# A decode kernel's second-layer queries spread between score groups, and one V half kept in the buffer

## The chip, the cores and the metric

The kernel runs on one core of a Trainium2 chip. The metric is device time in microseconds (us); lower is better. Kernels are compared only within the same rounds. A ratio is the mean time of one kernel's fast runs over that of the other's in the same rounds, so it is not quite the ratio of the medians that are quoted beside it.

## The reference, cut to what matters

Four blocks in a chain over eight batch rows, one token each: attention with a KV cache, an MLP block, and the same two again with the same weights and the same cache.

```python
def _A_ref(x, k_cache, v_cache, wq, wo):      # 8 rows, 16 query heads, 8 KV heads, 4096 keys, 256 wide
    q = (x @ wq) ...
    scores = einsum(q, k) * 256 ** -0.5
    o = einsum(softmax(scores), v)
    return o @ wo
x = x + A(layernorm(x));  x = x + B(layernorm(x))     # B: layernorm, two small MLPs
x = x + A(layernorm(x));  x = x + B(layernorm(x))     # the same K and V once more
```

One row's K for one head is 2 MiB, and so is its V. They are far too large to hold, and both layers need them, so loading them is the work.

## The kernel before

The cache goes through a buffer of 15 slots of 1 MiB; one load is "half" of a head's K or V. K of five heads per row (ten slots) is kept from the first layer to the second, so it is loaded and transposed once. V is loaded twice.

```python
KEEP_K = 5
KEEP_V = 0
NFILL = 2
...
def load_half(cache, b, h, half):
    i = free_slots.pop(0)
    ...  # one DMA of 1 MiB, waits for the last readers of slot i
...
def mid(b, first_head, heads):        # between the layers of one row
    mlp(x1T[:, :, b:b + 1], ...)      # x1T: the row after the first attention
    norm(x2T[:, :, b:b + 1], ...)
    groups = [[heads[0]], heads[1:]]  # query matmuls of head 1, then of the other seven
    for gr in groups:
        for h in gr: pe(lambda t, h=h: q_mms(t, range(4 * h, 4 * h + 4), 1, False), 16, ...)
        for h in gr: dv(...)          # copy the queries out of the bank psC
...
for b in range(B):
    mid(b, l2_heads[0], l2_heads + free_heads)
    if b + 1 < B: layer1(b + 1, free_heads[:NFILL])   # next row's heads 0, 1 fill the serial stretch
    layer2(b, l2_heads[:2])                           # kept heads 7, 6
    if b + 1 < B: layer1(b + 1, free_heads[NFILL:])   # next row's head 2
    layer2(b, l2_heads[2:])                           # kept heads 5, 4, 3
    layer2(b, free_heads)                             # cut: the last two rows order this differently
    if b + 1 < B: layer1(b + 1, kept_heads)           # next row's heads 3 to 7
```

A scheduler inside the kernel orders each engine's work once, at build time. The matmuls of `mid` have the highest priority, so PE does all of them before it turns to the first second-layer scores.

Of the kernel before, what the change touches and what calls it, by code (L numbers as in the profile page):

```python
# [18 lines left out]
RSQRT_MAGIC = 0x5F1FFFF9  # L19
RSQRT_STEPS = ((0.703952253, 1.681914091), (0.5, 1.5000003))  # L20
KEEP_K = 5
KEEP_V = 0
REP = 24
LAG = 1
NFILL = 2
FILL_EV = "ev"
PV0 = 128
PV1 = PV0 + DH
QW, HW, YW = 16, 24, 24
# [295 lines left out]
def bass_interleave_layers__gqa_block_cached__mixer_s_mlp__decode_kernel(  # L325
# [20 lines left out]
    plan = Plan()  # L346
# [72 lines left out]
    psC = nc.alloc_psum_tensor("psC", [P, 512], f32)  # L419
# [11 lines left out]
    def bcast(ap, shape, axis):  # L431

        dims = [list(x) for x in ap.ap]
        dims.insert(axis, [0, shape])
        return bass.AP(tensor=ap.tensor, offset=ap.offset, ap=dims)
# [8 lines left out]
    def dma_once(name, parts, keys, at):  # L444

        for i, (dst, src, nbytes) in enumerate(parts):
            dma(name, dst, src, nbytes, nc.alloc_semaphore(f"s_{name}{i}"), 16, [keys[i]],
                at - 0.5)
# [16 lines left out]
    YB = ["yb"]  # L465
# [12 lines left out]
    def const_b(gp):  # L478
# [5 lines left out]
            rd=["ident_f"], wr=["ident_b"])  # L484

    def const_c(v):
# [7 lines left out]
            wr=["sel"])  # L494

    for i in range(2):
        plan.op("dve", lambda v, i=i: v.memset(psS[i][:, PV0:PV0 + DH], 0.0), 0.3, "const",
                wr=[("pz", i)], banks=[("S", i)])
# [4 lines left out]
    def dv(fn, dur=0.13, rd=(), wr=(), banks=(), name="chain", prio=None):  # L503
        if prio is None:
            prio = CH + len(plan.ops)
        return plan.op("dve", fn, dur, name, rd=rd, wr=wr, banks=banks, prio=prio)

    def pe(fn, n, rd=(), wr=(), banks=(), name="chain", prio=None):
        if prio is None:
            prio = CH + len(plan.ops)  # L510
        d = 0.06 + 0.026 * n
        return plan.op("pe", fn, (d, d, 20 * n), name, rd=rd, wr=wr, banks=banks, prio=prio)
# [65 lines left out]
    def q_mms(t, mts, n, first):  # L578

        last = None  # L580
        w_ = QW if n == 1 else n
        for mt in mts:
            hq, c = mt // 2, mt % 2
            for kc in range(4):
                if kc < 3:
                    w = wq_sb[:, kc, hq * 256 + c:hq * 256 + 256:2]
                    r = yb[:, kc, 0:n]
                else:
                    o = (hq % 8) * 256
                    w = wqx_sb[:, o + c:o + 256:2]  # L590
                    r = yb[:, 3 if hq < 8 else 4, 0:n]
                if n == 1:
                    r = bcast(r, w_, 1)
                last = t.matmul(psC[:, mt * w_:(mt + 1) * w_], w, r, start=(kc == 0), stop=(kc == 3))  # L594
        return last

    WQ = ["wq0", "wq1", "wq2", "wqx0", "wqx1"]
# [62 lines left out]
    def flush(n):  # L660
        while len(pend) > n:
            pend.pop(0)()

    def pair(layer, b, h, kept_k, kept_v, keep_k, keep_v, lag=None):
# [126 lines left out]
        pend.append(back)  # L791
        flush(LAG if lag is None else lag)

# [22 lines left out]
                    wr=[("s", i, pc)], banks=[("T", bank)])  # L816
        a.tbank = v.tbank = bank

    def mid(b, first_head, heads):

        mlp(x1T[:, :, b:b + 1], ("x1", b), 1, x2T[:, :, b:b + 1], [("x2", b)])
        norm(x2T[:, :, b:b + 1], ("x2", b), 1, False)
        q = q2T[b % 2]
        groups = [[heads[0]], heads[1:]]
        for gr in groups:
            for h in gr:
                pe(lambda t, h=h: q_mms(t, range(4 * h, 4 * h + 4), 1, False), 16, rd=YB + WQ,
                   wr=["psC"], banks=["C"])
            lo, hi = min(gr), max(gr)
            for h in gr:  # L830
                dv(lambda v, h=h: v.tensor_copy(
                    q[:, 4 * h:4 * h + 4].rearrange("p (c j) -> p c j", c=2),
                    psC[:, 4 * h * QW:(4 * h + 4) * QW:QW].rearrange("p (j c) -> p c j", c=2)),
                   rd=["psC"], wr=[("q2", b, h)], banks=["C"])


    dma_once("x", [(x_row[:, 0:D], A_x[:, 0, :], 7168)], ["xr0"], 0)
# [1 line left out]
    def load_wq():  # L839
        dma_once("wq", [(wq_sb[:, kc, :], A_wq[kc * P:(kc + 1) * P, :], 1 << 20)  # L840
                        for kc in range(3)], ["wq0", "wq1", "wq2"], 2)
        dma_once("wqx", [(wqx_sb[0:64, :], A_wq[384:D, 0:2048], 1 << 19),
                         (wqx_sb[64:P, :], A_wq[384:D, 2048:4096], 1 << 19)], ["wqx0", "wqx1"], 2)

    def load_rest():
        dma_once("wo", [(wo_sb[:, 0:32 * D].rearrange("p (t n) -> p t n", n=D),
                         A_wo.rearrange("(t m) n -> m t n", m=P), 3670016)], ["wo0"], 6)
        dma_once("w3", [(w3_sb[:, kc, :], B_w3[kc * P:(kc + 1) * P, :], 458752)
                        for kc in range(3)], ["w30", "w31", "w32"], 18)
        dma_once("w3x", [(w3x_sb[0:64, :], B_w3[384:D, 0:896], 114688 * 2),  # L850
                         (w3x_sb[64:P, :], B_w3[384:D, 896:1792], 114688 * 2)], ["w3x0", "w3x1"], 18)
        dma_once("w4", [(w4_sb[:, 0:14 * D].rearrange("p (t n) -> p t n", n=D),
                         B_w4.rearrange("(t m) n -> m t n", m=P), 1605632)],
                 ["w40"], 20)
# [25 lines left out]
    free_heads = list(range(HKV - KEEP_K))  # L880
    kept_heads = list(range(HKV - KEEP_K, HKV))
    l2_heads = kept_heads[::-1]

    def layer1(b, heads):
        for h in heads:
            kk = h in kept_heads
            nv = KEEP_V if h == HKV - 1 else 0
            keep_v = [nv > 1, nv > 0]
            pair(0, b, h, None, None, yes if kk else no, keep_v)

    def layer2(b, heads):
        for h in heads:
            kk, kv = store.pop((0, b, h))
            pair(1, b, h, kk, kv, no, no)

    load_wq()
    load_rest()
    first_queries()
    layer1(0, free_heads + kept_heads)
    flush(0)  # L900
    for b in range(B):
        mid(b, l2_heads[0], l2_heads + free_heads)
        ev_eng[0] = FILL_EV
        if b + 1 < B:
            layer1(b + 1, free_heads[:NFILL])
        else:
            layer2(b - 1, free_heads)
        ev_eng[0] = "ev"
        layer2(b, l2_heads[:2])
        if b + 1 < B:  # L910
            layer1(b + 1, free_heads[NFILL:])
        layer2(b, l2_heads[2:])
        if b != B - 2:
            layer2(b, free_heads)
        if b + 1 < B:
            layer1(b + 1, kept_heads)
        flush(0)
# [4 lines left out]
    def ot(t):  # L922
        last = None
        for kc in range(4):
# [6 lines left out]
       rd=["psC"], wr=["o_row"], banks=["C"])  # L931
# [3 lines left out]
            wr=["done"], dma=(s_out, 16), prio=10 ** 6)  # L935
# [65 lines left out]
```

## Time and profile before

| | before |
|---|---|
| time, median of the first three runs | 1197.31 us |
| profiled span | 1196.5 us |
| HBM read | 463.54 MB, 432 loads of K and V |
| row period, from x1T to the next x1T, first six | 142.6 us |
| x1T to first second-layer scores | 22.4 to 25.3 us |

In the lines of the profile, PE is the matmul engine and PEld its loading of weights; DVE, ACT and POOL are the vector, scalar and GpSimd engines; SP issues the loads. L441 is line 441 of the kernel.

From the page of the kernel before: rate in 40 slices, bytes per queue, and what was read.

```profile
GB/s 348 409 398 418 320 413 416 417 414 348 417 416 418 385 372 417 418 416 359 390 416 417 418 325 401 417 415 418 346 417 417 417 399 350 417 417 366 345 415 155
q1 hardware_dynamic: 69344, 463.58, 96.1%
q8 instruction: 167, 2.74, 0.9%
HBM read 463.54 MB, written 0.01 MB: 387 GB/s over the span
```

The rate stands at 415 to 418 GB/s and falls once per row. That is a memory-bound kernel with eight dips. From the waits of the DMA queue (what the next load waited for; us in total, times, longest):

```profile
SPq L441 <- PE psS L697: 359.2, 117, 8.6
SPq L441 <- PE psS L737: 354.8, 141, 9.2
SPq L441 <- PE psT L805: 103.5, 50, 4.3
```

The loads wait for scores (L697) and value products (L737), which give slots back. Between the dips that costs nothing, since other loads are still in flight. In the dips it does. Here are ten-us windows of the second row, counted from x1T at 262.7 us; the columns are the length, the busy time of PE, PEld, DVE, ACT and POOL (with instructions), the granted clock, the DMA share (a packet counts whole where it starts, so 1.01 is possible) and GB/s.

```profile
252.70:262.70 10.00, 8.22 (x188) 6.03 (x186) 3.94 (x12) 1.23 (x5) 0.75 (x2) 1.00 1.01 415
262.70:272.70 10.00, 10.00 (x199) 9.89 (x198) 7.04 (x27) 3.50 (x7) 0.35 (x1) 1.00 0.96 377
272.70:282.70 10.00, 8.68 (x223) 7.81 (x222) 5.53 (x24) 2.02 (x10) 1.15 (x3) 1.00 0.85 287
282.70:292.70 10.00, 8.81 (x225) 7.33 (x221) 2.12 (x14) 0.76 (x5) 0.75 (x2) 0.53 0.99 373
292.70:302.70 10.00, 10.00 (x260) 8.73 (x256) 4.37 (x14) 2.79 (x8) 0.75 (x2) 0.96 1.00 415
```

In the dip PE is busy for 10.00 and then 8.68 of ten us: it transposes and scores the next row's first K halves and does the serial chain of norm, MLP, norm and queries. Slots come back when PE is done with their last readers. The timeline of the kernel before gives the two ends of the chain (start, length, engine, line, operation):

```profile
262.75 0.18 DVE L787 TENSOR_TENSOR x1T<-acc,psW 128x5 bf16<-128x5 f32 x1 [0.82 <-PE psW L775]
...
285.63 0.56 PE L697 MATMUL psS<-q2T,kv 128*128 128x48 bf16 x10
```

### The profile page before, as it was taken

Reading aid. Unit: us, or ns where it says so; the run is one execution under the profiler, and the core shown is the slowest. Engines: PE = TensorE matmul, PEld = TensorE weight load, DVE = VectorE, ACT = ScalarE, POOL = GpSimd, SP = SyncE. Lnnn points to the kernel's source line nnn. Section 1 sums busy time; section 2 is a strip of 40 time slices with the busy share of each in tenths; the row PEclk is TensorE's granted clock in tenths of the full one; section 3 lists DMA queues with packets and bytes.
Section 4 is the critical chain, followed back from the end, with each engine's and each line's share of the span. In section 5 each row is a group of like instructions: output and inputs, shape, how many; then the busy total and the mean of one; then the engine's idle time right before and its main releaser. Section 6 shows DMA issues by size and latency. Waiting matters only on the chain.

```text
span 1196.5 us, 46172 instructions
## 1 busy us (share of the span) xinstructions
PE 1005.6 (84%) x21301; PEld 861.9 (72%) x21301; DVE 509.1 (43%) x1632; ACT 274.3 (23%) x847; POOL 97.9 (8%) x270
## 2 busy tenths in 40 slices
PE   4878889889898887999789797888888888789787
PEld 4766877778677776777677686776877677678665
DVE  3433435444344443445344343444434453345333
ACT  0222213221132211332123211232223221132121
POOL 0000010000110011000110001000010000100110
PEclk9998889998899988999899988999889997899888
DMA  9999899999999999999999989999999999999893
GB/s 348 409 398 418 320 413 416 417 414 348 417 416 418 385 372 417 418 416 359 390 416 417 418 325 401 417 415 418 346 417 417 417 399 350 417 417 366 345 415 155
DMA packets 69536, 466.52 MB, mean 390 GB/s; under 512 B 7120, under 2 KB 13152, under 8 KB 13664
## 3 DMA queue, kind: packets, MB, share of 16 engines
q1 hardware_dynamic: 69344, 463.58, 96.1%
q8 instruction: 167, 2.74, 0.9%
q14 instruction: 25, 0.20, 0.0%
HBM read 463.54 MB, written 0.01 MB: 387 GB/s over the span
## 4 chain that ended last, share of the span: by engine, by line
PE 53%; DMA 34%; DVE 5%; issue 4%; SPq 3%; POOL 1%; ACT 0%
DMA kv<-in_A_v_cache_dram 20%; PE psT L805 18%; PE psS L697 14%; DMA kv<-in_A_k_cache_dram 14%; PE psS L737 8%; PE psW L775 4%; SPq L441 3%; PE psT L941 2%; DVE oS L751 2%; DVE oS L749 2%; PE psC L640 1%; PE psS L759 1%; PE psC L594 1%; PE psC L534 1%; PE psC L616 1%
## 5 line engine op out<-in xcount | busy, mean ns | idle before, releaser
L805 PE MATMUL psT<-ident_f,kv 128*128 128x128 f32 x2816 | 383.4, 284 | 11.4 <-DMA kv<-in_A_k_cache_dram 8.3
L805 PEld LDWEIGHTS psT<-ident_f,kv 128*128 128x128 f32 x2816 | 315.3, 145 | 25.6 <-DMA kv<-in_A_k_cache_dram 13.7
L813 DVE COPY kv<-psT 128x512 f32<-128x512 f32 x379 | 260.4, 691 | 171.2 <-PE psT L805 168.4
L814 ACT COPY kv<-psT 128x512 f32<-128x512 f32 x325 | 190.3, 586 | 517.9 <-PE psT L805 517.6
L737 PE MATMUL psS<-kv,pT 128*2 128x256 bf16 x4096 | 167.4, 289 | 45.2 <-DMA kv<-in_A_v_cache_dram 38.5
L697 PE MATMUL psS<-q2T,kv 128*128 128x48 bf16 x4096 | 145.6, 192 | 23.0 <-issue 22.8
L717 ACT ACTIVATE pT<-psS,nb 128x32 bf16<-128x32 f32 x256 | 73.2, 296 | 365.0 <-DVE nb L711 365.0
L697 PEld LDWEIGHTS psS<-q2T,kv 128*128 128x128 bf16 x4096 | 133.7, 103 | 31.7 <-issue 29.4
L697 PE MATMUL psS<-q1T,kv 128*128 128x48 bf16 x4096 | 143.2, 183 | 5.4 <-issue 4.9
L697 PEld LDWEIGHTS psS<-q1T,kv 128*128 128x128 bf16 x4096 | 130.1, 97 | 22.8 <-issue 17.6
L737 PEld LDWEIGHTS psS<-kv,pT 128*2 128x2 bf16 x4096 | 78.9, 85 | 75.5 <-DMA kv<-in_A_v_cache_dram 45.0
L709 POOL PARTITION_ALL_REDUCE gm<-pm x128 | 45.4, 354 | 893.5 <-DVE pm L707 845.6
L707 DVE TENSOR_REDUCE pm<-psS 128x2 f32<-128x64 f32 x128 | 28.7, 224 | 182.9 <-PE psS L697 182.2
L941 PE MATMUL psT<-ident_b 128*128 128x256 bf16 x614 | 100.3, 288 | 1.9 <-issue 1.9
L759 PEld LDWEIGHTS psS<-sel,oS 128*128 128x128 bf16 x512 | 23.9, 98 | 105.6 <-DVE oS L751 103.8
L775 PEld LDWEIGHTS psW<-oT,wo_sb 128*128 128x128 bf16 x2560 | 79.9, 97 | 23.2 <-DVE oT L765 11.9
L759 PE MATMUL psS<-sel,oS 128*128 128x2 bf16 x512 | 32.4, 167 | 74.7 <-DVE oS L751 67.7
L775 PE MATMUL psW<-oT,wo_sb 128*128 128x24 bf16 x2560 | 90.0, 183 | 6.0 <-issue 5.0
L749 DVE CAST oS<-psS 128x256 bf16<-128x256 f32 x128 | 54.1, 423 | 74.7 <-PE psS L737 72.3
L941 PEld LDWEIGHTS psT<-ident_b 128*128 128x128 bf16 x614 | 49.6, 100 | 22.9 <-issue 17.6
L722 POOL PARTITION_ALL_REDUCE Db<-rs x128 | 51.1, 399 | 173.4 <-ACT pT L717 173.4
L751 DVE TENSOR_TENSOR oS<-psS,oS 128x256 bf16<-128x256 f32 x128 | 54.3, 424 | 3.3
(83 smaller groups left out, 461.2 us busy)
## 6 DMA issues: line engine op xcount, KB each, us to landing
kv<-in_A_v_cache_dram SPq DMA_DIRECT2D x256, 1024.0 KB, 17.9
kv<-in_A_k_cache_dram SPq DMA_DIRECT2D x176, 1024.0 KB, 20.9
wo_sb<-in_A_wo_dram SPq DMA_DIRECT2D x1, 3584.0 KB, 32.9
wq_sb<-in_A_wq_dram SPq DMA_DIRECT2D x3, 1024.0 KB, 11.3
w_sb<-in_B_w_dram SPq DMA_DIRECT2D x1, 1568.0 KB, 23.8
w_sb<-in_B_w_dram SPq DMA_DIRECT2D x3, 448.0 KB, 24.4
wqx_sb<-in_A_wq_dram SPq DMA_DIRECT2D x2, 256.0 KB, 14.9
w3x_sb<-in_B_w_dram SPq DMA_DIRECT2D x2, 112.0 KB, 20.1
```

The source lines that it names most:

```text
L697: last = t.matmul(ps[:, 2 * i:2 * i + 2 * REP], a[:, c:256:2], bcast(rhs(c), REP, 1), start=(c == 0), stop=(c == 1))
L717: return a.activation(pT[nr][:, :, :].rearrange("p i j -> p j i")[:, jj, :], sview[:, jj, :], ACT.Exp, bias=nb[nr][:, jj:jj + 1], scale=IN ...
L722: plan.op("pool", lambda gp: gp.partition_all_reduce(Db[nr][:, :], rs[nr][:, :], P, RO.add), 0.5, "sum", rd=[("rs", nr, 0), ("rs", nr, 1)] ...
L737: last = t.matmul(ps[g4:g4 + 2, PV0:PV0 + DH], pT[nr][:, i, :], slot_ap(s_, s * 256, 256), start=(i < 4), stop=(i >= 28), skip_group_check ...
L749: plan.op("dve", lambda v: v.tensor_copy(oS[:, 0, :], po), 0.36, "o", rd=[("pv", par, x) for x in range(4)], wr=["oS0"], banks=[bk], prio=hi)
L751: plan.op("dve", lambda v: v.tensor_tensor(oS[:, 1, :], po, oS[:, 0, :], ALU.subtract), 0.36, "o", rd=["oS0"] + [("pv", par, x) for x in r ...
L759: last = t.matmul(ps[:, PV1 + 2 * c:PV1 + 2 * c + 2], oS[:, w, c * P:(c + 1) * P], sel[:, :], start=(w == 0), stop=(w == 1))
L775: last = t.matmul(psW[:, mt * YW:(mt + 1) * YW], dup(wo_sb, 2 * (2 * h + j) + c, mt), bcast(oT[nr][:, c, j:j + 1], YW, 1), start=(k == 0), ...
L805: last = t.transpose(psT[bank][:, s * P:(s + 1) * P], src, ident_f[:, :])
L813: return e.tensor_copy(dst, psT[bank][:, :])
L814: return e.copy(dst, psT[bank][:, :])
L941: last = t.matmul(psT[bank][:, 256 * i:256 * i + 256], ident_b[:, :], bcast(ident_b[:, :], 2, 1), start=True, stop=True)
```

## The change

The intent by its title is to shorten the chain: only two heads' queries (32 matmuls) are computed ahead of the first scores, and the other six heads' follow one by one between the score groups. The diff also sets `KEEP_V` to 1. The second V half of the last kept head (head 7) then stays in its slot until the second layer, which saves one load per row (424 loads instead of 432) and leaves four slots to rotate in the serial stretch instead of five.

```diff
-KEEP_V = 0
+KEEP_V = 1
+QFIRST = 2
...
-    def mid(b, first_head, heads):
+    def mid(b, heads):
         mlp(...)
         norm(...)
-        groups = [[heads[0]], heads[1:]]
-        ...  # all eight heads' matmuls, then their copies
+        for h in heads:
+            second_queries(b, h, None)          # 16 matmuls and a copy, as above
...
     def layer2(b, heads):
         for h in heads:
+            todo = q_todo.get(b, [])
+            for h2 in todo[:1 + (h in todo)]:
+                second_queries(b, h2, len(plan.ops))   # ordinary priority
+                todo.remove(h2)
             kk, kv = store.pop((0, b, h))
             pair(1, b, h, kk, kv, no, no)
...
-        mid(b, l2_heads[0], l2_heads + free_heads)
+        order2 = l2_heads + free_heads
+        mid(b, order2[:QFIRST])
+        q_todo[b] = order2[QFIRST:]
```

More of the change, by code (lines that the diff above doesn't have):

```diff
@@ L817, in transpose_piece, with second_queries @@
         a.tbank = v.tbank = bank
-    def mid(b, first_head, heads):
+    def mid(b, heads):
         mlp(x1T[:, :, b:b + 1], ("x1", b), 1, x2T[:, :, b:b + 1], [("x2", b)])
         norm(x2T[:, :, b:b + 1], ("x2", b), 1, False)
+        for h in heads:
+            second_queries(b, h, None)
+    def second_queries(b, h, prio):
         q = q2T[b % 2]
-        groups = [[heads[0]], heads[1:]]
-        for gr in groups:
-            for h in gr:
-                pe(lambda t, h=h: q_mms(t, range(4 * h, 4 * h + 4), 1, False), 16, rd=YB + WQ,
-                   wr=["psC"], banks=["C"])
-            lo, hi = min(gr), max(gr)
-            for h in gr:
-                dv(lambda v, h=h: v.tensor_copy(
-                    q[:, 4 * h:4 * h + 4].rearrange("p (c j) -> p c j", c=2),
-                    psC[:, 4 * h * QW:(4 * h + 4) * QW:QW].rearrange("p (j c) -> p c j", c=2)),
-                   rd=["psC"], wr=[("q2", b, h)], banks=["C"])
+        pe(lambda t: q_mms(t, range(4 * h, 4 * h + 4), 1, False), 16, rd=YB + WQ,
+           wr=["psC"], banks=["C"], prio=prio)
+        dv(lambda v: v.tensor_copy(
+            q[:, 4 * h:4 * h + 4].rearrange("p (c j) -> p c j", c=2),
+            psC[:, 4 * h * QW:(4 * h + 4) * QW:QW].rearrange("p (j c) -> p c j", c=2)),
+           rd=["psC"], wr=[("q2", b, h)], banks=["C"], prio=prio)
     dma_once("x", [(x_row[:, 0:D], A_x[:, 0, :], 7168)], ["xr0"], 0)
@@ L892, in layer2 @@
         for h in heads:
+            todo = q_todo.get(b, [])
+            for h2 in todo[:1 + (h in todo)]:
+                second_queries(b, h2, len(plan.ops))
+                todo.remove(h2)
             kk, kv = store.pop((0, b, h))
             pair(1, b, h, kk, kv, no, no)
+    q_todo = {}
     load_wq()
```

## The prediction

> **What bounds it now.** The page's rate row sits mostly at 415-418 GB/s, so one 1 MiB half of K or V costs 2.51 us. 466.5 MB at 418 GB/s are 1116 us of the 1196.5 us span; the other 80 us are start, tail and eight dips to 320-350 GB/s, one per row. In the windows of the second row the dip is 268-284 us (DMA share 0.84-0.93) and 289-293 us. The DMA queue's own waits name PE scores (359 us) and PE value products (355 us): loads wait for slots. In the dip, halves land 4.8 us after issue with an empty queue: 2.5 us of transfer and 2.3 us of fixed latency. The Trainium skill, "DMA: Bandwidth & Descriptors", section "Anatomy of one DMA", gives about 2.0 us fixed; the trace roughly agrees.
>
> The dip is the row's serial stretch: ten slots hold kept K, five carry the next row's first two heads while the chain norm, MLP, norm, queries runs. By the timeline x1T is written at 262.7, the first second-layer score starts at 285.8.
>
> **What the change does.**
> 1. Not named by its title: KEEP_V goes from 0 to 1. One V half per row (second half of the last kept head) stays resident. The load count falls from 432 to 424 halves: 8.4 MB, 20.1 us at full rate. It also leaves four rotating slots instead of five from the end of the first layer to that head's second-layer value product.
> 2. QFIRST: before, 16 query matmuls plus 112 more (2.96 us in the chain) precede the first scores. After, 16+16; the other six heads' 96 follow between score groups. By proportion the kept K slots of the first head come free about 2.5 us earlier. PE's total work is unchanged.
>
> **How much is on the path.** Before and after the dip DMA is saturated, so what counts is how far the load sequence has got. In the dip loads are slot-limited: one slot fewer delays each load to the next release, and one load fewer makes up for it. I moved the second row's landings by hand, keeping release times. Before, the last of nine loads following the fourth K half lands at 296.9 us (4.3 us lost); after, eight loads should land by about 294.8, 4.7 us lost. Gain 2.1 us. The third row gives about 1.8. Without QFIRST the next row's third K load would be issued as late as before (287.4) and part of this would be lost; with it DMA has no gap there. Some rows lose 1-2.5 us more 20 to 45 us after x1T; earlier release may recover 0.3 us per row. So about 2.3 us per row, 8 rows: 18 us. The shorter chain mostly pays for the lost slot.
>
> **Predicted: 1179 us**, 8 in 10 between 1170 and 1188. Faster by over 2% (under 1173.4) 0.18, within 2% 0.80, slower 0.02.
>
> **What would show it.** HBM read falls by 8.39 MB to about 455.2 MB. The dips are deeper (loads landing about 5 us after issue, four in a row) with about the same lost time; 415-418 GB/s elsewhere. First second-layer score about 21 us after x1T instead of 23-25. Row period from x1T to x1T down from about 142.5 to 140.2 us.
>
> **What would make it wrong.** If the dips do not deepen (releases come earlier than I kept them), up to 20 us plus the shorter chain would come through: 1165-1170. If four slots starve PE in the chain itself, so that scores of the next row's heads block the norm and query matmuls queued behind them, x1T to first score grows and the gain shrinks to under 8 us.

## The result

The changed kernel took 1188.34 us (median of four, 1186.89 to 1189.91); before took 1197.81 us in the same comparison. The ratio is 0.9921 with a 95% interval of 0.9904 to 0.9938. Right direction, half the gain forecast, just outside the range.

From the page of the changed kernel, the lines that answer to those of before:

```profile
GB/s 345 409 395 418 334 416 416 417 377 351 417 416 417 331 380 417 417 416 305 407 416 416 416 319 418 416 416 415 324 416 417 417 369 360 418 416 340 391 416 114
q1 hardware_dynamic: 68192, 455.19, 94.9%
q8 instruction: 167, 2.74, 0.9%
HBM read 455.15 MB, written 0.01 MB: 383 GB/s over the span
```

The waits of its DMA queue (lines have moved by one):

```profile
SPq L442 <- PE psS L698: 379.8, 128, 10.5
SPq L442 <- PE psS L738: 376.4, 142, 10.3
SPq L442 <- PE psT L806: 100.6, 43, 14.1
```

The windows of its second row, x1T at 260.8 us:

```profile
250.80:260.80 10.00, 6.75 (x115) 4.23 (x116) 2.28 (x9) 0.46 (x4) 0.40 (x1) 0.85 1.01 415
260.80:270.80 10.00, 10.00 (x195) 9.91 (x195) 6.84 (x25) 3.31 (x7) 0.35 (x1) 0.98 0.68 242
270.80:280.80 10.00, 9.01 (x241) 8.21 (x238) 5.88 (x28) 2.20 (x10) 1.15 (x3) 1.00 0.80 271
280.80:290.80 10.00, 9.45 (x266) 8.04 (x266) 2.69 (x15) 0.71 (x5) 1.11 (x3) 0.71 1.02 425
290.80:300.80 10.00, 8.99 (x184) 7.24 (x176) 4.83 (x12) 2.93 (x8) 0.75 (x2) 0.95 1.01 415
```

And the two ends of its chain in the timeline:

```profile
260.78 0.18 DVE L788 TENSOR_TENSOR x1T<-acc,psW 128x5 bf16<-128x5 f32 x1 [1.24 <-PE psW L776]
...
280.89 0.48 PE L698 MATMUL psS<-q2T,kv 128*128 128x48 bf16 x13
```

Two things happened. The chain is shorter: 22.9 us became 20.1 us (over the first seven rows 22.4 to 25.3 became 19.8 to 20.9 us; the granted clock over the 22 us after x1T was 0.89 to 1.00 in both, so it is not the cause), and the window 20 to 30 us after x1T is at the full rate instead of 373 GB/s. But the first ten us carry 242 GB/s instead of 377: 1.35 MB less, where one load is 1.05 MB. The bytes saved were not time saved; DMA stood still instead.

The 9.0 us between the two profiled spans divide as follows, from x1T to x1T: 0.7 us up to the first x1T, 4.2 us over the six full row periods (855.5 to 851.3 us), 3.2 us in the shorter seventh (113.2 to 110.0), and 0.9 us behind it (107.9 to 107.0). So a full row gained 0.7 us, where 2.3 us had been forecast. (Both kernels were traced a second time, in e12 and e5; with the two traces of each averaged it is 0.8 us.)

### The profile page after: what moved, and what is told of

It is laid out like the page before. It is cut to its first block, busy times and chain, and to the rows that moved or that the text cites. A ratio compares the mean times of both kernels' runs of the same rounds, so it can differ in the third digit from the quotient of the medians.

```text
span 1187.5 us, 46157 instructions
## 1 busy us (share of the span) xinstructions
PE 1011.8 (85%) x21297; PEld 863.7 (73%) x21297; DVE 514.2 (43%) x1635; ACT 273.9 (23%) x844; POOL 98.0 (8%) x270
## 3 DMA queue, kind: packets, MB, share of 16 engines
HBM read 455.15 MB, written 0.01 MB: 383 GB/s over the span
## 4 chain that ended last, share of the span: by engine, by line
PE 66%; DMA 18%; DVE 7%; issue 5%; SPq 3%; POOL 1%; ACT 0%
PE psT L806 22%; PE psS L698 18%; DMA kv<-in_A_v_cache_dram 14%; PE psS L738 10%; PE psW L776 5%; DMA kv<-in_A_k_cache_dram 4%; PE psT L950 3%; SPq L442 3%; DVE oS L752 3%; DVE oS L750 3%; PE psS L760 2%; PE psC L595 1%; PE psC L641 1%; PE psC L535 1%; PE psC L617 1%
## 5 line engine op out<-in xcount | busy, mean ns | idle before, releaser
L806 PE MATMUL psT<-ident_f,kv 128*128 128x128 f32 x2816 | 377.5, 282 | 6.3 <-DMA kv<-in_A_k_cache_dram 4.7
L738 PE MATMUL psS<-kv,pT 128*2 128x256 bf16 x4096 | 173.7, 291 | 49.3 <-DMA kv<-in_A_v_cache_dram 29.7
L698 PE MATMUL psS<-q2T,kv 128*128 128x48 bf16 x4096 | 149.1, 194 | 14.8 <-issue 14.6
L698 PEld LDWEIGHTS psS<-q2T,kv 128*128 128x128 bf16 x4096 | 137.4, 104 | 24.9 <-issue 22.3
L698 PEld LDWEIGHTS psS<-q1T,kv 128*128 128x128 bf16 x4096 | 129.5, 97 | 23.2 <-issue 16.7
L738 PEld LDWEIGHTS psS<-kv,pT 128*2 128x2 bf16 x4096 | 79.6, 85 | 85.2 <-DMA kv<-in_A_v_cache_dram 33.1
L776 PEld LDWEIGHTS psW<-oT,wo_sb 128*128 128x128 bf16 x2560 | 80.2, 97 | 23.0 <-DVE oT L766 10.5
L950 PEld LDWEIGHTS psT<-ident_b 128*128 128x128 bf16 x610 | 49.9, 101 | 22.2 <-issue 16.3
## 6 DMA issues: line engine op xcount, KB each, us to landing
wq_sb<-in_A_wq_dram SPq DMA_DIRECT2D x3, 1024.0 KB, 11.7
```

Of the source, the lines that this page charges most:

```text
L698: last = t.matmul(ps[:, 2 * i:2 * i + 2 * REP], a[:, c:256:2], bcast(rhs(c), REP, 1), start=(c == 0), stop=(c == 1))
L738: last = t.matmul(ps[g4:g4 + 2, PV0:PV0 + DH], pT[nr][:, i, :], slot_ap(s_, s * 256, 256), start=(i < 4), stop=(i >= 28), skip_group_check ...
L776: last = t.matmul(psW[:, mt * YW:(mt + 1) * YW], dup(wo_sb, 2 * (2 * h + j) + c, mt), bcast(oT[nr][:, c, j:j + 1], YW, 1), start=(k == 0), ...
L806: last = t.transpose(psT[bank][:, s * P:(s + 1) * P], src, ident_f[:, :])
L950: last = t.matmul(psT[bank][:, 256 * i:256 * i + 256], ident_b[:, :], bcast(ident_b[:, :], 2, 1), start=True, stop=True)
```

## The experiments

The first question was what each part of the change does alone, and what a slot is worth. My theory ("slot theory"): in the dip a load waits for a slot, so keeping a half removes one load and takes one slot, and the two cancel; only the shorter chain gains. The rival: the slot is cheap, and the deferred queries eat the gain.

In the table, times are us after x1T, means over the first six rows of one profiled run, worked out from the issue times and landing events in each trace: issue > last of the load's 16 landing events. h0 to h2 are the next row's heads in layer 1; h5 to h7 are kept heads in layer 2; between the last two loads of the table three are left out. Period is x1T to x1T. For a kernel traced twice, this is one of its traces and the other period stands in brackets.

| load, in order of issue | before | queries only (e6) | KEEP_V only (e9) | both (changed) | before, 14 slots (e3) | both, 16 slots (e4) |
|---|---|---|---|---|---|---|
| h1 K, 2nd half | -4.3 > 7.0 | -4.4 > 6.6 | -4.4 > 6.9 | -4.2 > 6.6 | -2.0 > 7.2 | -7.1 > 6.7 |
| h0 V, 1st | -2.2 > 9.6 | -2.2 > 9.2 | 4.6 > 10.0 | 4.8 > 9.7 | 4.7 > 10.2 | -4.0 > 9.2 |
| h0 V, 2nd | 4.8 > 12.3 | 4.6 > 11.6 | 9.1 > 14.0 | 9.3 > 14.2 | 9.2 > 14.0 | 4.9 > 11.7 |
| h1 V, 1st | 9.4 > 15.0 | 9.1 > 14.2 | 13.2 > 18.5 | 13.4 > 18.6 | 13.3 > 18.3 | 9.4 > 14.6 |
| h1 V, 2nd | 13.7 > 19.1 | 13.4 > 18.4 | 16.8 > 22.2 | 17.1 > 22.1 | 17.0 > 22.2 | 13.6 > 19.0 |
| h7 V, 1st | 17.4 > 22.4 | 17.1 > 22.1 | 17.3 > 25.1 | 17.5 > 25.2 | 17.5 > 25.4 | 17.4 > 22.3 |
| h7 V, 2nd | 18.2 > 25.7 | 17.7 > 25.4 | kept | kept | 18.4 > 28.0 | kept |
| h2 K, 1st | 18.9 > 28.4 | 18.3 > 28.0 | 18.4 > 27.8 | 18.3 > 28.1 | 25.4 > 31.1 | 17.9 > 25.5 |
| h2 K, 2nd | 25.7 > 31.5 | 21.8 > 30.6 | 25.0 > 30.8 | 21.8 > 30.6 | 27.2 > 34.1 | 18.6 > 28.3 |
| h6 V, 1st | 27.5 > 34.7 | 23.1 > 33.0 | 26.7 > 33.9 | 23.1 > 33.1 | 28.1 > 36.9 | 22.5 > 30.8 |
| h5 V, 1st | 34.7 > 45.1 | 30.8 > 43.1 | 34.0 > 44.2 | 31.1 > 43.1 | 34.3 > 47.0 | 30.3 > 40.8 |
| period | 142.6 (143.1) | 141.9 (142.3) | 142.1 (143.1) | 141.9 (142.2) | 145.0 | 139.3 |

### Each part alone, and a slot taken or given (e1 to e4)

e1 is the kernel before with `KEEP_V` alone:

```diff
-KEEP_V = 0
+KEEP_V = 1
```

> The kernel before with KEEP_V = 1 alone: 424 loads, four rotating slots in the serial stretch, queries all ahead of the first scores. Slot theory (the removed load is paid back by the lost slot because loads in the dip wait for slots): gain small, 1190 to 1197 us, lost DMA time per row from 10 us before to 45 us after x1T up by 1.5 to 2.5 us against before. Rival (the deferred queries are what costs, the slot is cheap): 1176 to 1183 us, faster than the changed kernel.

Measured: 1191.93 us against 1200.48 us of before on that chip, ratio 0.9936 (0.9910 to 0.9962). Its profiled run was its slowest of six. The DMA time lost from 10 us before x1T to 45 us after it (55 us less the bytes at 418 GB/s) was 6.6 and 6.8 us per row in the two traces of before, 9.4 in e1 and 8.3 in its repetition e9: up by 1.5 to 2.8 us, about as expected.

e2 is the changed kernel with `KEEP_V = 0`, so only the queries are deferred.

> The changed kernel with KEEP_V = 0: 432 loads, five rotating slots, deferred queries. Slot theory: the shorter chain releases the first kept K slots 2.5 us earlier, so part of the 1.3 us per row lost 20 to 45 us after x1T comes back: 1187 to 1194 us. Rival (deferred queries cost): 1197 us or more, and the first second-layer group is no earlier relative to x1T or later groups are late.

Measured: 1189.50 us, ratio 0.9915 (0.9891 to 0.9940): as much as the whole change.

e3 takes a slot from the kernel before and removes no load:

```diff
-HALVES = 15
+HALVES = 14
```

> The kernel before with 14 slots instead of 15: four rotating slots in the serial stretch with no load removed. Slot theory: each row loses nearly one load time (2.0 to 2.5 us) more in the dip, 1212 to 1219 us. Rival (a slot is cheap): 1197 to 1203 us.

Measured: 1219.92 us, ratio 1.0161 (1.0134 to 1.0188).

e4 gives the changed kernel a slot, at the cost of a wrong result on purpose (the record marks it "correct", but that is not claimed for it: its MLP reads the wrong weights, and the comparison with the reference let it through):

```diff
-HALVES = 15
+HALVES = 16
-w4_sb = sb("w4_sb", [P, 14 * D + 64], bf)
+w4_sb = wo_sb                       # and w4 is not loaded
```

> The changed kernel with 16 slots, the room taken from the second MLP weights, which are not loaded (they are read from the output projection's weights, so the result is wrong on purpose; 1.6 MB or 3.9 us of loading fall away once). Five rotating slots again with the load removed. Slot theory: the removed load comes through, row periods about 1.5 to 2.5 us shorter than in the changed kernel, 1167 to 1174 us in all. Rival (the gain is eaten elsewhere than in the dip): row periods as in the changed kernel, 1183 to 1186 us.

Measured: 1171.77 us, ratio 0.9762 (0.9738 to 0.9786). Some 3.8 us of this is the load that fell away once (1.6 MB at 418 GB/s; the first x1T comes at 115.3 instead of 119.2 us); the rest is put down to the slot.

Three of the four fell inside the range of the slot theory, and e3 0.9 us above its range, on a chip where before itself took 1200.48 us; none fell where the rival put it. The table shows why. With four rotating slots (changed, e9) the V halves go out at 4.8, 9.3, 13.4 and 17.1 us. With five (before, e6) they go out at -2.2, 4.8, 9.4 and 13.7 us. These are the same release times, shifted by one load. After the release at about 17 us the slots come in a row and DMA runs full again. The load that takes that release is followed by two more up to the first half of h2's K, both with a V half kept (h7 V, h2 K) and without (h7 V second half, h2 K). That half lands at 28.1 us and 28.0 us (28.3 and 28.4 us in the second traces, e5 and e2). A slot without its load (e3) moves that landing to 31.1 us, and a removed load without loss of a slot (e4) to 25.5 us: 2.7 us later and 2.6 us earlier, one load's time each.

The same windows from the second row of e6 (the same kernel as e2; x1T at 260.6 us) show the payback in bytes:

```profile
260.60:270.60 10.00, 10.00 (x194) 9.91 (x194) 6.82 (x25) 3.30 (x7) 0.35 (x1) 0.98 0.87 337
270.60:280.60 10.00, 9.01 (x242) 8.21 (x239) 5.88 (x28) 2.23 (x10) 1.15 (x3) 1.00 0.85 275
280.60:290.60 10.00, 9.49 (x266) 8.03 (x266) 2.70 (x15) 0.78 (x5) 1.11 (x3) 0.71 1.01 415
```

In the first 20 us this kernel moves 6.12 MB and the changed one 5.13 MB: 0.99 MB, the kept half, in the same 20 us. PE's and PEld's columns are the same in the second window, with and without the kept half, which fits PE setting the pace.

And from e3's second row (x1T at 265.9 us): the first window falls as in the changed kernel, without a load saved.

```profile
265.90:275.90 10.00, 10.00 (x198) 9.89 (x197) 7.08 (x27) 3.53 (x7) 0.35 (x1) 1.00 0.80 293
275.90:285.90 10.00, 9.01 (x242) 8.21 (x241) 5.75 (x26) 1.99 (x10) 1.15 (x3) 1.00 0.84 283
```

### Both against one, on one chip (e5, e6, e9)

e5 is the changed kernel again and e6 is e2 again, in the same rounds; e9 repeats e1.

> The changed kernel itself, once more, so that it is timed on one chip and in the same rounds as the one with deferred queries alone. Slot theory (the kept V half is fully paid back by its slot): the two within 3 us of each other, both 8 to 11 us under before. Rival (the two parts add up): the changed kernel at least 5 us under the one with deferred queries alone.

> Deferred queries alone (KEEP_V = 0), on the same chip as the changed kernel. Slot theory: within 3 us of the changed kernel. Rival: at least 5 us slower than it.

> KEEP_V = 1 alone, once more, because its first six runs spread over 8 us and its profile was of the slowest of them. Slot theory: the first K half of the next row's third head lands as late after x1T as in the kernel before (28.4 us, plus or minus 0.5), and the x1T to x1T period of the first six rows is that of before within 0.7 us; 1190 to 1199 us. Rival (one load fewer per row is worth its 2.5 us also with four slots): landing 2 us earlier, periods 2 us shorter, 1178 to 1184 us.

Measured: both 1190.82 us, ratio 0.9928 (0.9903 to 0.9953); queries only 1189.68 us, 0.9924 (0.9898 to 0.9949). With the queries deferred, the kept V half is worth nothing that these runs can tell (each interval is 3 us to either side; one load per row at full rate would be 20 us). `KEEP_V` alone gave 1193.22 us, 0.9967 (0.9930 to 1.0004); with e1 that makes 4 to 8 us, with wide intervals. In e9 h2's K lands 0.6 and 0.8 us earlier than in before, just past the 0.5 us that I had allowed, and in e1 0.1 us later and 0.2 us earlier. The two period means (143.1, 142.1) lie around those of before (142.6, 143.1), so no gain in the full rows stands out from what two traces of one kernel differ by. Part of it may be in the seventh period, 110.5 and 112.3 us against 113.2 and 111.8 us; that this is all is not shown.

### Smaller loads (e7, e8, e10, e11)

If slots are short, give them back in smaller pieces. e7 and e8 cut the same buffer into 30 slots of 512 KiB (e7 with `KEEP_V = 1`, e8 with 0):

```diff
-        i = free_slots.pop(0)
-        ...  # one DMA of 4096 columns
+        for w in range(2):
+            i = free_slots.pop(0)
+            ...  # one DMA of 2048 columns into quarter slot i
...
-            if not keep_k[j]: free_slots.append(ks[j])          # after both score groups of a half
+                if not keep_k[j]: free_slots.append(ks[j][qd])  # after each
```

> The changed kernel with the same buffer cut into 30 slots of half the size: a load is 512 KiB and a slot is given back as soon as its half of the scores or value products is done. Same bytes, same kept data. Slot theory: in the dip slots come back earlier and a load lands about 1.2 us sooner after issue, so 1.5 to 3 us per row less is lost: 1165 to 1178 us. Rival (the dip is set by the chain and by the fixed time of a load, which is now paid twice): no gain, 1185 to 1195 us.

> The same with KEEP_V = 0 (432 MiB loaded instead of 424). Slot theory: if the dip is now less slot-limited, the load that KEEP_V removes begins to come through, so this one is slower than its sibling with the kept V half, by 3 to 15 us; if the dip is as slot-limited as before, the two are equal.

Measured: 1207.29 us, ratio 1.0072 (1.0033 to 1.0111), and 1213.09 us, 1.0115 (1.0089 to 1.0141). Both are slower than either kernel, and e7 is slower than my range and the rival's. The page of e7 points to the reason:

```profile
GB/s 327 388 408 406 326 402 407 408 398 338 408 406 407 385 330 407 407 407 356 370 407 406 408 347 399 407 407 402 328 407 407 408 391 347 406 407 329 315 407 152
DMA packets 129442, 458.17 MB, mean 379 GB/s; under 512 B 13776, under 2 KB 19808, under 8 KB 128864
```

Outside the dips it holds 407 GB/s instead of 417: the packets are 4 KiB instead of 8 KiB and take 0.162 us (median) instead of 0.313 us, a little more than half. On 455 MB that is 27 us (455.15 MB at 407 less the same at 417 GB/s), where the median of e7 is 16 us above that of e5 in the same rounds. That the rate is the whole reason was not tested. The difference between e7 and e8 (6 us) would fit a kept V half that begins to pay with smaller slots, as the slot theory expected, but the two intervals overlap (1.0089 to 1.0111).

e10 and e11 therefore keep 15 full slots and 8 KiB packets, and split only the loads issued in the dip into two, each waiting only for the readers of its own half slot:

```diff
+SPLIT_V = ((0, 0), (0, 1), (1, 7))   # (layer, head)
+SPLIT_K = ((0, 2),)
...
+        n = 2 if split else 1
+        for w in range(n):
+            dma("kv", slot_ap(i, w * z, z), ..., slot_sem[i][w], ...)   # z = 4096 // n
```

> The changed kernel with full-size slots, but those loads that are issued in the dip (V of the next row's first two heads, V of the last kept head, K of the next row's third head) made as two loads of 512 KiB into the two halves of their slot, each waiting only for the readers of its own half. Slot theory: in the dip each half is issued 1 to 2 us earlier and lands 1.2 us sooner, while all other loads keep the full rate; lost time per row down by 1.5 to 3 us, 1168 to 1180 us. Rival (the dip is set by the chain of norm and MLP, not by slots): within 3 us of the changed kernel.

> The same with KEEP_V = 0. Slot theory: this too gains 1 to 3 us per row on deferred queries alone, 1168 to 1182 us; it ends near its sibling, the kept V half being worth at most what of the dip is no longer slot-limited. Rival: 1187 us or more.

Measured: 1199.08 us, ratio 1.0011 (0.9980 to 1.0043), and 1197.15 us, 0.9987 (0.9959 to 1.0016). My expectation failed for both. The rival's failed for e10 (within 3 us of the changed kernel) and held for e11 (1187 us or more). Both lost the gain. In e11's trace the first pieces do go out earlier than the whole loads of e6 (of h1's first V half at 6.7 instead of 9.1 us, of its second at 10.5 instead of 13.4 us; means of rows two to six), but h1's V is complete at 17.8 us instead of 18.4 us, and the second half of h2's K at 32.0 us instead of 30.6 us. Later the second half of h2's V goes out at 34.0 us instead of 28.9 us. The schedule is built anew for each kernel, so the split is not the only difference, and I have not separated the two.

### Once more before, and one head ahead (e12, e13)

> The kernel before itself, for a second trace of it, since row periods of one kernel differ by 0.3 to 1 us between two profiled runs. If the reading of the first trace is not chance: x1T period of the first six rows 142.3 to 143.0 us, third-head K half landing 28.2 to 28.8 us after x1T, the 16 loads behind the first V half of the fifth head taking 40.5 to 40.9 us by their last ring (41.2 to 41.4 us in the kernels with deferred queries). If it is chance, the 16 loads take 41.2 us or more here too.

> Deferred queries with QFIRST = 1 (one head's queries ahead of the first scores instead of two), KEEP_V = 0. If the gain comes from the length of the chain ahead of the first scores, 16 query matmuls fewer give about 0.4 us per row by proportion, 2 to 3 us in all against deferred queries alone, so 1185 to 1188 us where that one has 1189.5. If what is left of the dip is set by slot releases inside the chain and by the late ring after it, no change: 1188 to 1191 us.

e12 is the kernel before: 1199.79 us, ratio 1.0009 (0.9986 to 1.0032) to its own other runs, first-six period 143.1 us. (In the expectation above, "ring" is a landing event.) The period and the landing of h2's first K half (28.8 us) came out at the upper edge of what I expected. e13 changes `QFIRST` from 2 to 1 in e2: 1196.21 us, ratio 0.9974 (0.9950 to 0.9998). That is worse than two heads ahead, and the expectation failed: its first second-layer scores are no earlier (20.1 to 21.9 us after x1T, against 19.8 to 20.9 us in the changed kernel), h2's first K half lands at 29.4 us, and its period is 143.1 us. So fewer queries ahead of the first scores is not always a shorter way there.

The trace of e13 also shows where the shorter chain gains, by the mean of the 16 landing events. From h2's first K half to h5's first V half, six loads on, takes 15.2 us in e13 and in all five other traces with deferred queries (changed, e2, e4, e5, e6), but 16.5 and 16.7 us in the two traces of before and 16.3 us in e1 and e9. Six loads in a row are 15.1 us. So deferring the queries closes a hole of 1.1 to 1.5 us behind h2's first K half (e3, where that half lands 2.7 us later, takes 15.5 us). e13 closes it too, but loses 1.0 us before it: inside the dip the loads go out 0.7 to 1.1 us later than in e6 (h0's second V half goes out at 5.3 instead of 4.6 us, h1's at 9.8 and 14.1 instead of 9.1 and 13.4, h2's first K half at 19.4 instead of 18.3). Why they do is open.

e12 settles something else. By the landing of h5's V, 43 to 45 us after x1T, the changed kernel is 1.9 us ahead of before. At the next x1T it is 0.7 us ahead. The loss lies where DMA is saturated in both:

| | before | before (e12) | both | both (e5) | queries only (e6) |
|---|---|---|---|---|---|
| next 16 loads after h5's first V half, by the last of 16 landing events | 40.6 | 40.5 | 41.4 | 41.4 | 41.4 |
| the same, by the mean of the 16 events | 40.55 | 40.53 | 40.62 | 40.62 | 40.62 |
| last event behind the mean, h5 V | 1.5 | 1.6 | 1.4 | 1.4 | 1.2 |
| last event behind the mean, head 7's last V half in layer 1 | 2.1 | 2.2 | 2.9 | 3.0 | 2.8 |

The bytes arrive as fast as before, but the last of the 16 parts of a load is later. By the mean of the 16 events the changed kernel is 1.8 us ahead at h5's V and still 1.7 us at head 7's last V half in layer 1 (135.5 instead of 137.2 us after x1T); by the last event it is 1.9 and then 0.9 us ahead (138.4 instead of 139.3). The Trainium skill, "DMA: Bandwidth & Descriptors", section "Why a DMA increments its semaphore by 16 and not by 1", says that a load runs on up to 16 DMA engines that finish independently, and that only the full 16 means all of it has landed. This trace agrees: the events of one load are 2 to 5 us apart late in a row. In the dip, where the queue runs dry, the laggard catches up; the spread of a load in the changed kernel's second row falls from 5.0 us to 0.6 us there. The next x1T waits for the last part of the last V half, so 0.8 to 0.9 us of the gain goes to the laggard. The two traces of before agree on this, and so do the three of deferred queries in the table (and e2, with 41.2 us for the 16 loads), so it is not the chance of one trace. Why the lag grows more when the DMA queue fills earlier is open.

## Why the prediction was wrong

- **"In the dip loads are slot-limited: one slot fewer delays each load to the next release, and one load fewer makes up for it."** Right: h2's first K half lands at 28.1 us in the changed kernel and at 28.0 us with the queries alone; e3 and e4 show each side by itself.
- **"Gain 2.1 us ... So about 2.3 us per row, 8 rows: 18 us."** This is the step that failed, in its size. The hand-moved landings compared before as measured, with a step of 3.8 us in that row between two landings that follow one another in a filled queue (22.1 and 25.9 us after x1T), with an idealised after: its end fits steps of 2.5 us each. The eighth load was to land 32.1 us after x1T (294.8 less 262.7); it landed at 33.0 us in that row and 33.1 us on average. So the gain there was 1.2 us in that row instead of 2.1, 1.1 us in the third instead of 1.8, and 1.5 us on average. The missing part is the last of a load's 16 parts: by the mean of the 16 events the changed kernel's last steps in that row are indeed 2.5 to 2.6 us, by the last event they are 2.5, 3.6, 2.5 and 2.5 us.
- **"The shorter chain mostly pays for the lost slot."** Wrong way round, and it follows from the first bullet: if the removed load makes up for the slot, the chain's gain is free. e5 and e6 show that it is the whole gain as far as they can tell: 1189.68 us without the kept half, 1190.82 us with it.
- **"Before and after the dip DMA is saturated, so what counts is how far the load sequence has got."** Incomplete, and this is the other half of the miss. The rate is the same, but a load counts as landed with its last part. The 1.9 us gained by h5's V shrank to 0.9 us by the last V half of the row, almost wholly through the laggard, and to 0.7 us by the next x1T. Why the laggard falls further behind in the changed kernel stays open.
- **The chain.** "About 2.5 us earlier" and the first score "about 21 us after x1T" were close: 20.1 us in the second row, and h2's second K half goes out at 21.8 instead of 25.7 us, 3.9 us earlier.
- **What would show it.** HBM read fell by 8.39 MB as said. Loads in the dip land 4.9 to 5.2 us after issue, four in a row, as said. "About the same lost time" was off: forecast were 0.4 us more than before (4.7 instead of 4.3), and by the landing of h6's V it was 1.0 us more on average (one load of 2.5 us fewer, 1.5 us earlier). Against e6, which has the same chain, the removed load's 2.5 us were lost in full. The period was to be 140.2 us; it was 141.9 and 142.2 us.
- **What would make it wrong.** Neither of the two cases named came about: the dips did deepen, and x1T to first scores shrank.

## What to carry to other kernels

In the dip of this kernel, where loads wait for buffers, keeping data to save a load was an even trade: the buffer it occupied cost as much time as the load saved. So before counting a kept buffer as free, look whether loads wait for slots there. Test such a change in parts, since here one part of the change did all the work and the other added nothing to it, while their sum looked like a modest success of both. And when moving landing times by hand, compare estimate with estimate or measurement with measurement; an ideal "after" against a measured "before" hands the difference between the two to the change. What the consumer waits for is the last part of a load, so that is the landing to move.

## What the Trainium skill lacked or had wrong

- "DMA: Bandwidth & Descriptors", section "Anatomy of one DMA — SWDGE (gpsimd) path", gives about 2.0 us of fixed time per load for loads issued by GpSimd. The page has no such total for loads issued from SP, as all are here: in the dip a 1 MiB load into a queue run nearly empty took 4.9 to 5.2 us from issue to its last landing event, so 2.4 to 2.7 us beyond the 2.51 us of transfer.
- The same page has no figure for how far apart the 16 parts of one load land in a long stream of loads: late in a row the first and the last event of one load were 4.2 us (before) to 5.0 us (changed) apart on average, and it did not close while the queue was full.
- "Runtime: NRT & Kernel Launch", section "Instruction fetch mechanics", says that instructions come in 16 KiB blocks by DMA and that this is mostly hidden. The traces agree on the size (167 packets of 16,384 bytes on the queue named instruction), but each takes 1.07 us (median), as long as 3.4 packets of 8 KiB at 0.313 us. Together they are 0.9% of the 16 engines. The traces tie them to the drift, though no run varied them: from 35 us after x1T to the end of a row, the first event of a load gets 0.07 to 0.08 us further ahead of the mean of the 16 from one load to the next when an instruction packet starts between them, and 0.01 to 0.02 us when none does (before and changed, 97 steps with a packet and some 170 without in each).
- "Perfetto Trace Analysis", section "Optimization Strategy", says that a gap which repeats can mean too few buffers. Agreed, and it can be put in numbers here: one slot moves the landing behind the dip by 2.6 to 2.7 us and the row period by 2 to 3 us (e3 145.0 against 142.6 and 143.1 us, e4 139.3 against 141.9 and 142.2 us).
